# Five weight stages beside the attention's memory, and an expert's weight conversions inside its branch

## The chip, the cores and the metric

One core of one Trainium2 chip runs the whole program in a single launch. The metric is device time in microseconds (us); lower is better. Engines are named as in the profile: PE (matmul) and PEld (weight load), DVE, ACT, POOL, and SP, which issues most DMAs.

## The reference

Three stages follow each other. A windowed attention over 4 batches, 8 heads and 512 local plus 32 global positions gives 2176 tokens of 512 features. A token-shift feed-forward block turns them into `y`. Then comes a mixture of 8 experts, and this is the stage that the change is about:

```python
for b in range(B):
    prev_e = -1
    for s in range(S):
        fresh_e = int(np.argmax(logits[b, s]))
        if s == 0 or local_gate[b, s] < 0.5: e = fresh_e
        else: e = prev_e if prev_e >= 0 else fresh_e
        prev_e = e
        ...                              # p = softmax(logits[b, s])
        h = np.maximum(x[b, s] @ w1[e], 0.0)
        out[b, s] = p[e] * (h @ w2[e])
```

Each expert has `w1` (512x1024) and `w2` (1024x512), together 4 MB in float32.

## The kernel before

Every matmul is made of three passes (`mm3`, L19 to L24): the operands are split into a high part and a rest, and high*high, high*rest and rest*high are summed. So each weight must be converted before it is used. Eight pieces of 512 KB make one expert's weights: pieces 0 to 3 are `w1`, 4 to 7 are `w2`. A piece is loaded by SP into a stage (`part`, L770; a tile of 128x1024), ACT copies it to the high part (L779), and DVE, or POOL for pieces 3 and 7 of each expert (`PP`, L35), subtracts to get the rest (L782). Then the stage is free and SP loads the next piece into it: `whole` and `step` do one conversion and one such load. A load waits on SP until the subtraction of the stage's last piece is done, and SP takes its loads in program order. In what follows `Pk` is the k-th piece, counted over all experts: P8 to P15 belong to the second expert (expert 1), P16 to P23 to expert 2, P24 to P31 to expert 3, and so on.

Three stages (`st0` to `st2`, L1070) lie in a pool on the right side that opens when attention is done (`late`, L727). Two more (`sw0`, `sw1`, L852) are allocated in `alloc`, after the second stage of the program, and SP loads them first inside `run` (`s.fetch()`, L1012). Expert 0's eight pieces are converted during the feed-forward block, so the expert stage begins with P8 to P10 in `st` and P11, P12 on their way to `sw`.

While expert e is computed, expert e+1's eight pieces are converted:

- Experts 0 and 1 run `one` (L941), for one chunk of 128 tokens. `tall` (L899) computes the hidden layer with tokens as the stationary operand: two halves `b`, each 12 matmuls; the relu of a half (L918) goes to `hs`, `turn` transposes it back (L904) and ACT and DVE evacuate it (L906, L907). Conversions stand at `TW`: three before the first half (L909), one after its relu (L919), one at the turn inside the second half (L915). The other three go into `product` (L923), after steps 2, 4 and 6 of 8.
- Experts 2 to 6 run `expert` (L961). Nested branches on the token count `c` pick a side: `joined(N)` computes N=256, 288, 320 or 352 tokens at once, `big` 256 and then more, `single` one chunk, `none` nothing. Behind the branches stands a common tail (L998 to L1000): a `product` of 24 matmuls with bank 0. Five conversions stand in the side, three of them in `wide` (L887, after the relus of steps 2, 4, 6 by `FW`) and two in the next products, and three in the tail (L999). In the profiled execution the relus' shapes show that expert 2 runs `joined(288)`, experts 3 and 4 run `big`, expert 5 `joined(352)` and expert 6 `joined(256)`.
- Expert 7 runs `one` without conversions.

Inside the expert stage each engine's order is the order of the program text. Each engine evaluates the branches itself. PE's sequencer runs ahead of its array: it executes a branch while matmuls that stand before it are still queued.

Of the kernel before, what the change touches and what calls it, by code (L numbers as in the profile page):

```python
# [10 lines left out]
F32=mybir.dt.float32; F32R=mybir.dt.float32r; BF=mybir.dt.bfloat16; I32=mybir.dt.int32  # L11
AF=mybir.ActivationFunctionType; ALU=mybir.AluOpType; X=mybir.AxisListType.X
PSUM=bass.MemoryType.PSUM; DRAM=bass.MemoryType.DRAM
P=128; D=512; F=1024; E=8; SG=32; SL=512; S=544; NB=4; T=2176; HD=64; NK=9; NCH=17
# [4 lines left out]
def mm3(nc,out,wh,wl,xh,xl,first,last,order=None):  # L19

    i=nc.tensor.matmul(out,wh,xh,start=first,stop=False)  # L21
    if order: order(i)
    nc.tensor.matmul(out,wh,xl,start=False,stop=False)  # L23
    return nc.tensor.matmul(out,wl,xh,start=False,stop=last)  # L24
# [7 lines left out]
GA=6; PA=6  # L32
ND=[k for k,n in enumerate([1, 5, 5, 11, 3, 4, 6, 16]) for _ in range(n)]
V7=[1,1,2,2,3,3,3,3]
PP=(0,0,0,1,0,0,0,1); TW=(1,1,1,(2,4,6),3)  # L35
NR=4; NP=4
FX=(3,5,7); WJ=(288,320,352); MW=352; FW=(2,4,6); NW=(2,3); NST=2
def tiles(n): return 4*n-3
LAT=0.2; DLAT=2.1; SLACK=dict(P=0.15,A=0,D=0,G=0)
def op(e,d,need=(),free=(),when=None): return e,d,need,free,when  # L40
# [1 line left out]
class Sched:  # L42
# [11 lines left out]
    def one(s):  # L54

        for x in sorted(s.L,key=lambda x:(s.t<x[3]+(SLACK.get(x[2][0],0) if x[4] else 0),x[0])):
            e,d,need,free,when=x[2]
            if x[3]>s.t or (e and s.busy[e]>s.t) or any(s.places[k]<need.count(k) for k in need) or (when and not when()): continue
            for k in need: s.places[k]-=1
            if e:  # L60
                end=s.t+d; s.busy[e]=end; later=end+(DLAT if e in "QW" else LAT)
                s.left+=[(later,k) for k in free]
            s.next(x)
            if e: same=x[2] and x[2][0]==e; x[3]=end if same else later; x[4]=not same
            return True
# [686 lines left out]
class Experts:  # L752
# [19 lines left out]
    def split(s,e,which,q,st,pool=False):  # L772
# [4 lines left out]
        else:  # L777
            yield "A",.95
            nc.scalar.activation(h[:,qs],st,AF.Copy)  # L779
        if not pool: pool=PP[4*which+q]  # L780
        yield ("G",2.46) if pool else ("D",1.14)
# [67 lines left out]
    def alloc(s):  # L849
        w=s.work  # L850

        new=[s.xwork.tile([P,1024],F32,name=f"sw{i}",bufs=1) for i in range(NST)]  # L852
        s.x=[[s.xwork.tile([P,4,512],F32R,name=f"x{q}{i}",bufs=1) for q in "hl"] for i in range(2)]
        s.h=[w.tile([P,8,MW],F32R,name=f"h{q}",bufs=1) for q in "hl"]
        s.at=w.tile([P,2],I32,name="at",bufs=1); s.by=w.tile([P,2],F32,name="by",bufs=1)
        s.bank=[s.ps.tile([P,512],F32,tag=f"po{i}",name=f"po{i}",bufs=1) for i in range(2)]
        s.st+=new; s.free+=new
    def rows(s,i,n=256): return [t[:,:,i[1]:i[1]+n] for t in s.x[i[0]]]
    def row(s,e,k):

# [26 lines left out]
    def wide(s,i,e,N,W=(),X=()):  # L887

        nc=s.nc; W=list(W); X=list(X); w1h,w1l=s.views(e,0); xh,xl=s.rows(i,N); hh,hl=[t[:,:,:N] for t in s.h]
        for f in range(8):  # L890
# [4 lines left out]
            nc.vector.scalar_tensor_tensor(out=hl[:,f],in0=ph,scalar=0.0,in1=hh[:,f].bitcast(F32),op0=ALU.max,op1=ALU.subtract)  # L895
            if f in FX: s.go(X)
            if f in FW: s.go(W)
        s.go(X,8); s.go(W,8)
    def tall(s,i,e,W=(),X=None):  # L899

        nc=s.nc; W=list(W); w1h,w1l=s.views(e,0); xh,xl=s.rows(i); hh,hl=s.h
        def turn(b):
            pt=s.ps.tile([P,4,P],F32,tag="ph",name="pht2",bufs=4)
            for f in range(4): nc.tensor.transpose(pt[:,f],hs[b][:,f*P:(f+1)*P],s.ident)  # L904
            sl=slice(4*b,4*b+4)
            nc.scalar.activation(hh[:,sl,:P],pt,AF.Copy)  # L906
            nc.vector.tensor_sub(hl[:,sl,:P],pt,hh[:,sl,:P].bitcast(F32))  # L907
        hs=[]
        s.go(W,TW[4])  # L909
        for b in range(2):  # L910
            ph=s.ps.tile([P,512],F32,tag="ph",name="pht",bufs=4)
            bs=slice(b*512,(b+1)*512)
            for d in range(4):
                if b and d==2:
                    turn(0); s.go(W,TW[1])  # L915
                mm3(nc,ph,xh[:,d,:P],xl[:,d,:P],w1h[:,d,bs],w1l[:,d,bs],d==0,d==3)
            hs.append(s.work.tile([P,512],F32,tag="osb",name="hs",bufs=2))
            nc.scalar.activation(hs[b],ph,AF.Relu)  # L918
            if b==0: s.go(W,TW[0])  # L919
        if X is None: return lambda: turn(1)  # L920
        for f in X: f()
        s.go(W,8); turn(1)
# [18 lines left out]
    def one(s,i,e,b,W,X,o=None):  # L941

        W=list(W); last=s.tall(i,e,[W.pop(0) for _ in range(min(5,len(W)))])
        g=dict((f,[]) for f in range(8)); g[TW[2]].append(last)
        for f,x in zip((0,3,4),X): g[f].insert(0,x)
        for f,w in zip(TW[3],W): g[f].append(w)
        s.product(b,e,slice(0,P),g); s.place(b,*s.cols(e,0),o=o)
    def more(s,i,e,k,c,d=0):

# [10 lines left out]
            with two.Else(): single()  # L960
    def expert(s,i,i2,e,c,rows,own,X,third):  # L961

        tc=s.tc; keep=s.loaded,list(s.staged),list(s.free); W=[s.whole]*5
        def begin(k=0,early=True):
            s.loaded,s.staged,s.free=keep[0],list(keep[1]),list(keep[2])
            ch=e*NCH+s.o[e]+2*k
            s.nc.gpsimd.tensor_copy(s.at,s.idx[:,ch:ch+2]); s.nc.gpsimd.tensor_copy(s.by,s.pcol[:,ch:ch+2])
            if early: rows()
        def second(W): s.product(1,e,slice(P,2*P),dict(zip((0,2),([w] for w in W))))
        def big():  # L970
            begin(1,False)
            s.wide(i,e,256,W[:3],[own,lambda: (rows(),X[0]()),X[1]])
            s.out_(0,e,0,slice(0,P),{2:W[:1]}); s.out_(1,e,1,slice(P,2*P),{2:W[:1]})
            with tc.If(c>=tiles(4)) as four:
                s.wide(i2,e,256); second([])
            with four.Else(): s.tall(i2,e,[],[])
        def joined(N):
            begin()
            s.wide(i,e,N,W[:3],X)
            if N>256: s.out_(0,e,2,slice(256,N))  # L980
            second(W[:2])
        def single():
            begin(); s.tall(i,e,W,X)
        def none():
            begin()
            for g in (*W,*X): g()
        L=WJ
        def chain(k):
            if k==len(L): big(); return
            with tc.If(c>=tiles(3)+k+1) as up: chain(k+1)  # L990
            with up.Else(): joined(L[k])
        with tc.If(c>=tiles(2)) as two:
            with tc.If(c>=tiles(3)) as up: chain(0)
            with up.Else(): joined(256)
        with two.Else():
            with tc.If(c>=1) as some: single()
            with some.Else(): none()
        s.place(1,s.by[:,1:2],s.at[:,1:2])  # L998
        s.product(0,e,slice(0,P),{1:[third],2:[s.whole],4:[s.whole],6:[s.whole]})  # L999
        s.place(0,s.by[:,0:1],s.at[:,0:1])  # L1000
    def run(s):
        tc=s.tc; K=s.K
# [52 lines left out]
def program(tc,ins,out):  # L1055
    nc=tc.nc
    with ExitStack() as ctx:
        p=lambda n,**k: ctx.enter_context(tc.tile_pool(name=n,bufs=1,**k))
        const=p("const")
        y=p("dram",space=DRAM).tile([T+1,D],F32,name="y")  # L1060
        ident=const.tile([P,P],F32,name="ident"); make_identity(nc,ident)
        pair=lambda pool,i: [pool.tile([P,4096],F32R,tag=f"slot{i}{q}",name=f"slot{i}{q}") for q in "hl"]
        wp=p("wp"); slots=[pair(wp,0)]
        early=[wp.tile([P,4096],t,tag="slot1"+q,name="early"+q) for q,t in (("h",I32),("l",F32))]
        def place():
            slots.append(pair(wp,1)); return slots[1]
        x=Experts(tc,ident,ins['moe2_w1'],ins['moe2_w2'],y,out,slots)
        def right():
            r=p("right",side="right")
            x.st=[r.tile([P,1024],F32,name=f"st{i}") for i in range(3)]  # L1070
            x.xs=[r.tile([P,2,D],F32,name=f"xs{i}") for i in range(x.K)]
            t=pair(r,2); x.free=list(x.st); x.fetch(); return t
        with ExitStack() as st:
            m=phase1(tc,st,ins,const,y,ident,x,slots,early,place,right)
            x.idx,x.pcol,x.counts,x.cmax=m.idx,m.acc[:,E*NCH:],m.ci,m.cm

        t=dict(reuse_waits="tile")
        x.xwork=p("xwork",**t); x.work=p("work",**t); x.ps=Pools("pt",p("pst",space=PSUM,**t),p("ps2",space=PSUM,**t))
        x.alloc()
        slots.append(pair(p("wq",**t),3))  # L1080
        with tc.manual_schedule():
            x.run()
# [23 lines left out]
```

## Time and profile before

| | |
|---|---|
| three runs | 773.02, 768.14, 772.2 us (median 772.2) |
| the profiled execution | 773.22 us, of which its span is 771.5 us |
| mean granted TensorE clock | 0.973 |
| PE busy | 94% of the span |
| DVE, ACT, POOL busy | 64%, 51%, 45% |
| DMA | 99 GB/s over the span |
| loads of expert weights | 42 into `st`, 22 into `sw` |

The span is the time from the first to the last instruction. PE is busy nearly all the time, so a change shows in the stretches in which it is not. The chain of waits that ended last covers only the last microseconds here and says nothing on the expert stage, so the idle entries on PE's own timeline are read instead, and what each of them waited for. Attention and the feed-forward block fill the first 535 us, the experts the rest.

### The profile page before, as it was taken

The page shows a single profiled execution, that of the slowest core. Times are in us where ns is not written, and L with a number is a line of the kernel's source. Part 1 is how long each engine was busy: PE and PEld are TensorE (multiplying, and loading weights), DVE is VectorE, ACT ScalarE, POOL GpSimd, SP SyncE. Part 2 cuts the span into 40 slices and gives each one's busy share as a digit, 9 for nine tenths or more (in the row PEclk, how much of TensorE's full clock was granted, in tenths as well). Part 3 has the DMA queues.
Part 4 walks back from the last instruction along what each step waited for, and adds up shares of the span by engine and source line. Part 5 has one row for each costly group of instructions (what it writes and reads, how often), then busy time and mean ns, then how long its engine had stood idle before and what let it go on. Part 6 is the DMA issues. An engine that isn't in the chain of part 4 may idle for free. (4 is left out here: it accounts for less than half of the span.)

```text
span 771.5 us, 13972 instructions
## 1 busy us (share of the span) xinstructions
PE 726.4 (94%) x4702; PEld 611.4 (79%) x4702; DVE 496.9 (64%) x1477; ACT 389.9 (51%) x974; POOL 345.0 (45%) x480
## 2 busy tenths in 40 slices
PE   5888888999999999999999899999989999999997
PEld 3555676889898888898888789777777998889795
DVE  6698878968578587587675693577754624435361
ACT  4787566665265565464664442243643613334251
POOL 5566858644626346437245251211643422404421
PEclk9997799999999999999999999999999999999999
DMA  6585133121210321211110320042884633606530
GB/s 150 134 239 147 58 77 107 42 66 23 65 43 3 79 53 24 73 37 40 42 24 14 123 83 28 19 146 65 314 292 137 240 120 109 205 30 193 165 129 24
DMA packets 93185, 76.37 MB, mean 99 GB/s; under 512 B 70350, under 2 KB 74446, under 8 KB 93074
## 3 DMA queue, kind: packets, MB, share of 16 engines
q1 hardware_dynamic: 89618, 64.27, 28.0%
q0 software_dynamic: 3456, 10.75, 4.1%
q8 instruction: 53, 0.87, 0.5%
q14 instruction: 58, 0.48, 0.2%
HBM read 66.08 MB, written 9.44 MB: 98 GB/s over the span
## 5 line engine op out<-in xcount | busy, mean ns | idle before, releaser
L223 POOL TENSOR_SCALAR pl<-pl,mx 128x192 f32<-128x192 f32 (+1 forms) x128 | 64.0, 512 | 86.1 <-DVE mx L220 40.5
L217 ACT ACTIVATE pl<-pl,mx 128x224 f32<-128x224 f32 (+1 forms) x128 | 58.8, 461 | 34.8 <-DVE mx L214 28.0
L21 PE MATMUL psk<-xs,slot0h 128*128 128x256 f32 x256 | 74.6, 297 | 0.8 <-ACT xs L447 0.8
L23 PE MATMUL psk<-xs,slot0h 128*128 128x256 f32 x256 | 73.6, 289 | 0.0
L24 PE MATMUL psk<-xs,slot0l 128*128 128x256 f32 x256 | 73.4, 288 | 0.0
L449 POOL TENSOR_TENSOR xs<-xm,xs 128x512 fp32r<-128x512 f32 (+1 forms) x36 | 46.7, 1309 | 40.2 <-ACT xs L447 40.2
L894 ACT ACTIVATE hh<-ph 128x256 fp32r<-128x256 f32 (+2 forms) x56 | 22.4, 400 | 76.3 <-PE ph L24 45.9
L442 POOL TENSOR_SCALAR xm<-xT,mut 128x256 f32<-128x256 f32 (+7 forms) x96 | 42.7, 461 | 36.8 <-DVE xT L293 17.9
L21 PE MATMUL psv<-slot1h,kh 128*128 128x512 f32 x136 | 55.3, 406 | 0.0
L23 PE MATMUL psv<-slot1l,kh 128*128 128x512 f32 x136 | 54.3, 400 | 0.0
L24 PE MATMUL psv<-slot1h,kl 128*128 128x512 f32 x136 | 54.2, 398 | 0.0
L895 DVE SCALAR_TENSOR_TENSOR hl<-ph,hh 128x256 fp32r<-128x256 f32 (+2 forms) x56 | 24.7, 442 | 44.2 <-ACT hh L894 42.2
L229 PE MATMUL ptp<-ident,pl 128*128 128x128 f32 x256 | 44.1, 292 | 6.8 <-DVE qT L120 1.3
L21 PEld LDWEIGHTS psk<-xs,slot0h 128*128 128x128 f32 x256 | 48.9, 194 | 1.8 <-ACT xs L447 0.9
L23 PEld LDWEIGHTS psk<-xs,slot0h 128*128 128x128 f32 x256 | 48.9, 191 | 1.2
L24 PEld LDWEIGHTS psk<-xs,slot0l 128*128 128x128 f32 x256 | 48.9, 191 | 0.6
L237 PE MATMUL av<-ph,v 128*128 128x256 f32 x192 | 44.7, 293 | 2.2 <-DVE xT L293 1.8
L866 POOL DMA_INDIRECT xs<-y,idx x23 | 24.8, 1078 | 46.9 <-PE pt L873 22.4
L445 DVE SCALAR_TENSOR_TENSOR xm<-xT,mut,xm 128x256 f32<-128x256 f32 (+7 forms) x96 | 41.4, 464 | 3.2 <-POOL xm L442 3.0
L120 DVE TENSOR_TENSOR plo<-ptp,ph 128x512 fp32r<-128x512 f32 x48 | 32.7, 685 | 14.9 <-ACT ph L118 14.7
L21 PE MATMUL ph<-xh,slot2h 128*128 128x256 f32 (+1 forms) x128 | 37.9, 296 | 4.2 <-issue 4.2
L229 PEld LDWEIGHTS ptp<-ident,pl 128*128 128x128 f32 x256 | 30.6, 148 | 13.8 <-issue 3.3
(740 smaller groups left out, 2396.5 us busy)
## 6 DMA issues: line engine op xcount, KB each, us to landing
st<-in_moe_w_dram SPq DMA_DIRECT2D x42, 512.0 KB
sw<-in_moe_w_dram SPq DMA_DIRECT2D x22, 512.0 KB
y<-r SPq DMA_DIRECT2D x17, 256.0 KB
qn<-in_q_l_dram SPq DMA_DIRECT2D x32, 128.0 KB
kn<-in_k_l_dram SPq DMA_DIRECT2D x32, 128.0 KB
earlyh<-in_moe_w_k_dram SPq DMA_DIRECT2D x8, 512.0 KB
raw<-in_moe_w_v_dram SPq DMA_DIRECT2D x8, 512.0 KB
vn<-in_v_l_dram SPq DMA_DIRECT2D x24, 96.0 KB
```

Of the source, the lines that this page charges most:

```text
L21: i=nc.tensor.matmul(out,wh,xh,start=first,stop=False)
L23: nc.tensor.matmul(out,wh,xl,start=False,stop=False)
L24: return nc.tensor.matmul(out,wl,xh,start=False,stop=last)
L120: nc.vector.tensor_sub(out[1],x,out[0].bitcast(F32))
L217: nc.scalar.activation(p[:,h,ks],p[:,h,ks],AF.Exp,bias=mx[:,h:h+1],scale=-1.0,accum_out=mx[:,4+h:5+h])
L223: nc.gpsimd.tensor_scalar(out=p[:,h,ks],in0=p[:,h,ks],scalar1=mx[:,6+h:7+h],scalar2=0.0,op0=ALU.mult,op1=ALU.add)
L229: nc.tensor.transpose(pt[:,c,h],p[:,h,c*96:c*96+P],s.ident)
L237: nc.tensor.matmul(o,s.v(u,x,i,c),P_[y][:,c],start=c==m==0,stop=c==1 and m==len(parts)-1)
L442: nc.gpsimd.tensor_scalar(out=x[:,u,o:o+k],in0=s.xT[b][:,c,q:q+k],scalar1=m[:,1,c:c+1],scalar2=0.0,op0=ALU.mult,op1=ALU.add)
L445: nc.vector.scalar_tensor_tensor(out=x[:,u,o:o+k],in0=s.xT[b][:,c,1+q:1+q+k],scalar=m[:,0,c:c+1],in1=x[:,u,o:o+k],op0=ALU.mult,op1=ALU.add)
L449: nc.gpsimd.tensor_sub(xl[:,cs,:n],x[:,:,:n],xh[:,cs,:n].bitcast(F32))
L866: s.nc.gpsimd.indirect_dma_start(out=s.xs[i][:,j,:],out_offset=None,in_=s.y,in_offset=IndirectOffsetOnAxis(ap=s.idx[:,ch:ch+1],axis=0))
```

## The change

- `NST` stages are no longer allocated in `alloc`. All five lie in the right pool, so all five are loaded as soon as attention is done. When the expert stage begins, P8 to P12 are staged, and `run`'s `fetch` has nothing to do.
- Expert 1's `tall` converts one piece at its start, one after the first half's relu, two at the turn and one after the second half's relu, instead of three, one and one. Expert 0's places stay.
- All eight conversions of experts 2 to 6 stand inside the side. `wide` has places after steps 1, 2, 4, 6 and 7: five are taken by `joined(256)`, four by the wider ones, three by `big`. The rest go into the products of the side. The tail keeps only the preparation of a token chunk (`third`).

```diff
-PP=(0,0,0,1,0,0,0,1); TW=(1,1,1,(2,4,6),3)
+PP=(0,0,0,1,0,0,0,1); TW=((3,1,1,0),(1,1,2,1)); TF=(2,4,6)
-FX=(3,5,7); WJ=(288,320,352); MW=352; FW=(2,4,6); NW=(2,3); NST=2
+FX=(3,5,7); WJ=(288,320,352); MW=352; FW=(1,2,4,6,7); NST=2
...
-        new=[s.xwork.tile([P,1024],F32,name=f"sw{i}",bufs=1) for i in range(NST)]
-        s.st+=new; s.free+=new
...
-        s.go(W,TW[4])
+        n=TW[e>0]
+        s.go(W,n[0])
...
-                    turn(0); s.go(W,TW[1])
+                    turn(0); s.go(W,n[2])
...
-            if b==0: s.go(W,TW[0])
+            s.go(W,n[1+2*b])
...
-        tc=s.tc; keep=s.loaded,list(s.staged),list(s.free); W=[s.whole]*5
+        tc=s.tc; keep=s.loaded,list(s.staged),list(s.free); W=[s.whole]*8
-        def second(W): s.product(1,e,slice(P,2*P),dict(zip((0,2),([w] for w in W))))
+        def second(W): s.product(1,e,slice(P,2*P),{0:W[:1],1:W[1:2],2:W[2:]})
-            s.out_(0,e,0,slice(0,P),{2:W[:1]}); s.out_(1,e,1,slice(P,2*P),{2:W[:1]})
+            s.out_(0,e,0,slice(0,P),{0:W[:1],2:W[:1],4:W[:1]}); s.out_(1,e,1,slice(P,2*P),{0:W[:1],2:W[:1]})
-            s.wide(i,e,N,W[:3],X)
-            if N>256: s.out_(0,e,2,slice(256,N))
-            second(W[:2])
+            s.wide(i,e,N,W[:5 if N==256 else 4],X)
+            if N>256: s.out_(0,e,2,slice(256,N),{0:W[:1],2:W[:1],4:W[:1]})
+            second(W[:3 if N==256 else 1])
-        s.product(0,e,slice(0,P),{1:[third],2:[s.whole],4:[s.whole],6:[s.whole]})
+        s.product(0,e,slice(0,P),{1:[third]})
...
-            x.st=[r.tile([P,1024],F32,name=f"st{i}") for i in range(3)]
+            x.st=[r.tile([P,1024],F32,name=f"st{i}") for i in range(3+NST)]
```

## Rows read from the trace of the kernel before

**Rows 1.** PE's timeline, expert stage: start us, duration us, instruction, [idle before <-releaser]

```profile
555.98 0.65 PE L904 MATMUL pht<-ident,hs 128*128 128x128 f32 x4 [1.84 <-ACT slot2h L779]
560.58 0.66 PE L904 MATMUL pht<-ident,hs 128*128 128x128 f32 x4 [0.54 <-ACT hs L918]
569.08 0.58 PE L21 MATMUL ph<-xh,slot2h 128*128 128x288 f32 x1 [2.77 <-issue]
...
695.74 0.40 PE L21 MATMUL ph<-xh,slot1h 128*128 128x352 f32 x1 [0.35 <-issue]
...
730.77 0.39 PE L21 MATMUL ph<-xh,slot2h 128*128 128x256 f32 x1 [1.41 <-issue]
```

**Rows 2.** PE's branch instructions by line: duration ns min/median/max, first and last start us

```profile
L990 PEldq COMPARE_BRANCH  x1: 5790/5790/5790, 563.1 to 563.1; - x1
L990 PEldq COMPARE_BRANCH  x1: 3700/3700/3700, 591.2 to 591.2; - x1
L990 PEldq COMPARE_BRANCH  x1: 3913/3913/3913, 691.7 to 691.7; - x1
L990 PEldq COMPARE_BRANCH  x1: 3679/3679/3679, 719.0 to 719.0; - x1
L993 PEldq COMPARE_BRANCH  x1: 5532/5532/5532, 725.2 to 725.2; - x1
```

**Rows 3.** Busy by stretch: us, engines (instructions), granted clock, DMA share, GB/s

```profile
568.90:572.20 3.30, 3.12 (x13) 3.15 (x14) 0.00 (x0) 0.00 (x0) 2.86 (x5) 0.50 0.90 283
591.00:595.00 4.00, 4.00 (x19) 3.24 (x18) 0.85 (x1) 0.00 (x0) 3.98 (x2) 1.00 0.06 14
596.00:600.00 4.00, 4.00 (x21) 3.25 (x21) 2.10 (x3) 2.62 (x4) 1.02 (x1) 1.00 0.95 317
564.00:568.00 4.00, 2.31 (x11) 1.56 (x9) 3.26 (x5) 2.60 (x3) 2.79 (x3) 1.00 1.03 409
724.00:728.00 4.00, 4.00 (x21) 3.28 (x20) 2.09 (x4) 2.78 (x4) 1.03 (x1) 1.00 0.89 226
```

**Rows 4.** DMA queues, 563.2 to 566.45, 566.45 to 567, 592 to 593: packets, MB, share

```profile
q1 hardware_dynamic: 412, 1.29, 99.0%
...
q8 instruction: 1, 0.02, 12.0%
...
q8 instruction: 1, 0.02, 8.8%
```

**Rows 5.** DMA queues, 725.3 to 728.1, then 728.1 to 728.2

```profile
q1 hardware_dynamic: 154, 0.57, 87.6%
...
q8 instruction: 1, 0.02, 55.8%
```

**Rows 6.** SP's timeline: weight loads before the entry of expert 6

```profile
722.99 2.18 SPq L770 DMA_DIRECT2D sw<-in_moe_w_dram  x2
```

**Rows 7.** ACT's timeline, expert 1

```profile
554.38 1.06 ACT L779 ACTIVATE slot2h<-st 128x1024 fp32r<-128x1024 f32 x1 [2.68 <-DMA st<-in_moe_w_dram]
555.34 0.58 ACT L918 ACTIVATE hs<-pht 128x512 f32<-128x512 f32 x1
...
558.98 1.06 ACT L779 ACTIVATE slot0h<-st 128x1024 fp32r<-128x1024 f32 x1 [1.35 <-DMA st<-in_moe_w_dram]
559.95 0.58 ACT L918 ACTIVATE hs<-pht 128x512 f32<-128x512 f32 x1
...
561.27 0.60 ACT L906 ACTIVATE hh<-pht 128x512 fp32r<-128x512 f32 x1 [0.25 <-PE pht L904]
```

**Rows 8.** ACT's timeline, experts 2 (to 597.87) and 5

```profile
583.16 1.05 ACT L779 ACTIVATE slot1h<-sw 128x1024 fp32r<-128x1024 f32 x1
...
584.76 1.05 ACT L779 ACTIVATE slot1h<-sw 128x1024 fp32r<-128x1024 f32 x1
585.71 1.05 ACT L779 ACTIVATE slot3h<-st 128x1024 fp32r<-128x1024 f32 x1
...
597.87 2.00 ACT L779 ACTIVATE slot3h<-st 128x1024 fp32r<-128x1024 f32 x2
...
710.72 1.05 ACT L779 ACTIVATE slot2h<-st 128x1024 fp32r<-128x1024 f32 x1
```

**Rows 9.** POOL's and DVE's timelines, subtractions that overlap

```profile
550.80 2.43 POOL L782 TENSOR_TENSOR slot3l<-st,slot3h 128x1024 fp32r<-128x1024 f32 x1
...
550.75 4.70 DVE L782 TENSOR_TENSOR slot2l<-sw,slot2h 128x1024 fp32r<-128x1024 f32 x2
```

More of the change, by code (lines that the diff above doesn't have):

```diff
@@ L943, in one @@
         W=list(W); last=s.tall(i,e,[W.pop(0) for _ in range(min(5,len(W)))])
-        g=dict((f,[]) for f in range(8)); g[TW[2]].append(last)
+        g=dict((f,[]) for f in range(8)); g[1].append(last)
         for f,x in zip((0,3,4),X): g[f].insert(0,x)
-        for f,w in zip(TW[3],W): g[f].append(w)
+        for f,w in zip(TF,W): g[f].append(w)
         s.product(b,e,slice(0,P),g); s.place(b,*s.cols(e,0),o=o)
```

## The prediction

> **What bounds the kernel now.** PE is busy nearly all the time, so I read its own timeline in the expert stage first, for every idle entry over 0.3 us. There are five [rows 1]. Two stand in expert 1 (1.84 and 0.54 us) and end with ACT's conversion or the relu behind it. Three stand at the first matmul after a branch: at the entry of expert 2 (2.77 us), of expert 5 (0.35 us) and of expert 6 (1.41 us). Their releaser is "issue", that is, no semaphore. Together they are 6.91 us, 0.9% of the span.
>
> So the second view is PE's branch instructions [rows 2]. Those shown jump, and the sequencer gets its next instructions after 3.7 to 5.8 us. PE hides this as long as queued matmuls last. Branch time less idle time gives how long they last: 5.79-2.77 = 3.0 us, 3.91-0.35 = 3.6 us, 5.53-1.41 = 4.1 us. The jumps out of a side at 591.2 (3.70 us) and 719.0 (3.68 us) leave no idle entry.
>
> Third, why a jump takes 3.7 us or 5.8 us. Where DMA was nearly idle, 591 to 595 with a share of 0.06 [rows 3], the instruction queue's packet came between 592 and 593 and the jump of 591.2 took 3.70 us. At 563.1 the loads' queue took 99% of the DMA engines' time and no instruction packet came until after 566.45 [rows 4]; the jump was done 2.4 us after that. At 725.2 it was the same: no packet until 728.1 [rows 5], and two weight loads had been issued just before, from 722.99 to 725.2 [rows 6]. I read this so: an instruction fetch stands behind the loads issued before it. Two loads then hold a fetch for 5.1 us after the first one's issue (728.1-722.99), and PE has its instructions 2.4 us later. The idle time at 569.08 also costs clock: from 568.9 to 572.2 the granted clock was 0.50, the lower level of 1.2 GHz [rows 3], so at most half of 3.3 us, 1.65 us.
>
> **The change part by part.**
>
> *Five stages early.* Two 512 KB loads move from the start of the expert stage to the end of attention. P11 and P12 need no wait at expert 0, but no idle PE entry stands there, so this is worth nothing by itself. The two loads stand on SP ahead of nothing that is due then; I take 0. Phase one's order may shift with them; no row prices that, and I allow 1 us either way.
>
> *Expert 1.* ACT's third conversion at the start waits 2.68 us for its load [rows 7], and the first half's relu, which is ready, is queued behind it (555.34). PE waits for that relu, 1.84 us. With one conversion at the start the relu runs in time and this wait goes. Likewise the fifth conversion now waits 1.35 us for its load ahead of the second relu, and PE waits 0.54 us; after the change it stands behind that relu. What is late next: this fifth conversion (P20) still waits for its load, which lands at about 559, because its stage is freed by POOL in expert 0 and that does not move. Behind it ACT queues the next chunk's evacuation and the second turn's evacuation (561.27), and the product's fifth step needs the latter. The chain is 558.98 + 1.06 + 0.59 + 0.60 = 561.2, against 561.87 now [rows 7]. So of 2.4 us I count 0.7 us as a gain by the end of expert 1. Bounds: 0 and 2.4.
>
> *Entry of expert 2.* Expert 1's later pieces load as before and the DMA engines are full (share 1.03 from 564 to 568 [rows 3]); the fetch stands behind the same loads and PE only reaches the branch earlier. So I count the 0.7 us as the whole gain of experts 0 and 1 together, if PE starts expert 2 0.7 us sooner, and nothing for the 2.77 us. Bounds: 0, and all of 1.84+0.54+2.77+1.65 = 6.8 us.
>
> *The tail without conversions.* Expert 2's tail now starts its three conversions at 597.87 [rows 8]; in the change they run earlier. Before the entry of expert 5 no load is in flight: 0.35 us goes. Before the entry of expert 6, of the two loads from 722.99 one remains (P55's stage comes from POOL after the scatter, as P51's does now), so the fetch is held about half as long and 1.41 us goes. Sum 1.76 us. Bounds: 0 and 1.76.
>
> *The sides with conversions.* ACT does not wait for PE between conversions. In expert 2 the third one starts at 583.16, and two follow at once from 584.76 on [rows 8]. After the change the fourth stands at 583.16 (step 6 of `wide`), and four more run back to back, 0.95 us apart, until about 588.6. The fourth is POOL's: it subtracts from 584.2 to 586.6, 2.43 us. DVE does not get on beside it: two subtractions that started with POOL's took 4.70 us, 2.43 plus two of 1.1 [rows 9]. So stages come free at 586.6, 587.7, 588.8 and 590.0, and four loads (2.1 MB) stand ahead of the jump at 591.2. Now the DMA engines are idle there, with the share of 0.06. Price: two loads hold a fetch 5.1 us; two more at the 317 GB/s of 596 to 600 [rows 3] add 3.3 us. The fetch comes at 586.6+8.4 = 595.0, PE has its instructions at 597.4, the jump takes 6.2 us, and with matmuls for 4.1 us the new idle time is 2.1 us. In expert 5 the fourth conversion stands at 710.72; loads go out at 714.2, 715.3, 716.4 and 717.5; 714.2+8.4+2.4 = 725.0 against 719.0+4.1: 1.9 us. Sum 4.0 us. Lower bound: all four at 409 GB/s [rows 3] and 1 us to start, 6.1 us, which gives 0 at both. Upper bound: at 226 GB/s, 10.2 us, 3.9+3.7 = 7.6 us, and twice 1.65 us if the clock falls: 10.9 us. I take the middle rate, as it is that of loads into freed stages in this very expert. `big` converts at least 15 us before its exit; no price. `joined(256)` loads no further expert; no price.
>
> The DMA engines' order is what the sum hangs on. The Trainium skill (DMA: Bandwidth & Descriptors, "Queues, rings and completion order") says that each DMA engine goes round its queues packet by packet. By that rule a fetch would not stand behind loads, and the sum would be that of rival three. The gaps without a packet in [rows 4, 5] speak against it.
>
> *Sum.* -0.7 - 1.76 + 4.0 = +1.5 us. The profiled execution took 773.22 us, with a span of 771.5, so it becomes 774.7 with a span of 773.0; the median of the runs is 1.0 us lower, so 773.7 us. A measurement here tells about 1%, 7.7 us, from no change.
>
> **The rivals.** One: *everything goes and the exits stay hidden.* PE gains 6.8+1.76 = 8.6 us: 763.6 us. For it: the removed waits are on PE itself. Against it: the load of P20 and the full DMA engines up to 575 do not change. It needs expert 1's loads to land about 3 us sooner.
>
> Two: *the exits become the bound*, slower than before. It decides from about 3 us of idle time each, where the clock falls too, as it did after 2.77 us but not after 1.84 us: 10.9-1.76 = +9.1 us, 781.3 us. For it: 226 GB/s was seen with loads into the same kind of stage. Against it: nothing else is on the queues at 591 and 719.
>
> Three: *the fetch does not stand behind the loads.* Then neither the entries gain nor the exits lose; only the 0.7 us of expert 1 remains: 771.5 us.
>
> Four: *exits hidden, expert 1 as I have it*: -0.7-1.76: 769.7 us. For it: at 409 GB/s the price is 0.
>
> **How the numbers follow.** Forecast 0.45, rival one 0.12, two 0.08, three 0.15, four 0.20. The likeliest is 773.7 us, with its own range of 771 to 777. Leaving out one and two, which are 0.2 together, the range is 767.0 to 778.5: rival four less a part of the entry's 2.77 us, and the forecast with the exits' upper price but no fall of the clock, 773.7+3.6, and 1 us for phase one. Faster by over 1% (below 764.5) is rival one alone, 0.12; slower by over 1% is rival two, 0.08; the rest, 0.80, is within 1%.
>
> **What the profile would show.** Right: the 1.84 us entry gone, and PE's idle entries at experts 5 and 6 gone, with their jumps near 3.7 us; new idle entries of about 2 us at the first matmul of the tails of experts 2 and 5, with jumps near 6 us and a DMA share near 1 there. Wrong: exits that still take 3.7 us beside loads in flight (the reading of the queue falls), expert 2's entry without idle time (the loads were not the limit), or stretches before 535 us that differ by over 1 us.

## Result and profile after

| | before | after |
|---|---|---|
| median (range) of 17 runs each, us | 770.97 (765.42 to 775.4) | 777.9 (773.48 to 783.24) |
| ratio | | 1.0093, 95% interval 1.0072 to 1.0114 |
| profiled execution, us (span) | 773.22 (771.5) | 779.77 (778.0) |

The ratio is a loss of about 7.2 us (0.0093 x 771), between 5.6 and 8.8. Forecast were +1.5 us and 773.7 us, with a range of 767.0 to 778.5: the time lies inside the range and within 1%, but close to the upper edge, and above the 771 to 777 of the likeliest case.

Spans can't be compared here: the first matmul of the expert stage stands at 532.0 to 538.7 us in the executions shown here, with hardly a difference in the program ahead of it. So I cut the expert stage at the first matmul of experts 2, 3, 5, 6 and 7 on PE's timeline and compare its parts (us). Each row is one execution, and the idle time before a cut counts to the part ahead of it:

| kernel | experts 0, 1 | 2 | 3, 4 | 5 | 6 | 7 to end | stage |
|---|---|---|---|---|---|---|---|
| before | 32.31 | 32.26 | 94.40 | 35.03 | 23.08 | 17.65 | 234.73 |
| after | 32.97 | 34.75 | 94.23 | 35.47 | 27.31 | 17.69 | 242.42 |
| early stages alone | 32.63 | 32.37 | 94.37 | 34.25 | 23.07 | 17.64 | 234.33 |
| conversions in the sides alone | 31.38 | 32.88 | 94.21 | 34.47 | 27.47 | 18.23 | 238.64 |
| after, tail as before | 32.89 | 32.38 | 94.25 | 35.28 | 23.07 | 18.27 | 236.14 |
| after, half loads | 30.73 | 31.19 | 94.19 | 33.59 | 27.39 | 17.76 | 234.85 |
| after, three conversions less | 33.62 | 34.42 | 94.51 | 34.41 | 23.08 | 18.02 | 238.06 |
| dense | 32.49 | 31.13 | 94.24 | 33.70 | 23.09 | 17.95 | 232.60 |
| dense exits only | 33.31 | 32.36 | 94.40 | 33.64 | 27.47 | 17.50 | 238.68 |

The stage is 7.69 us longer after the change: 4.23 in expert 6, 2.49 in expert 2, 0.66 in experts 0 and 1, 0.44 in expert 5. PE's timeline, as in [rows 1], names the places (lines after the change stand one or two lower: the branch of L990 is L989):

```profile
559.54 0.50 PE L21 MATMUL po<-slot3h,hh 128*128 128x512 f32 x1 [0.30 <-ACT hh L904]
561.98 0.80 PE L24 MATMUL po<-slot3h,hl 128*128 128x512 f32 x1 [1.71 <-DVE hl L905]
568.58 0.41 PE L21 MATMUL ph<-xh,slot2h 128*128 128x288 f32 x1 [2.02 <-issue]
...
597.24 0.47 PE L21 MATMUL po<-slot0h,hh 128*128 128x512 f32 x1 [2.13 <-issue]
...
697.56 0.40 PE L21 MATMUL ph<-xh,slot1h 128*128 128x352 f32 x1 [0.18 <-issue]
...
726.93 0.47 PE L21 MATMUL po<-slot3h,hh 128*128 128x512 f32 x1 [1.76 <-issue]
...
753.19 0.77 PE L21 MATMUL po<-slot0h,hh 128*128 128x512 f32 x1 [2.59 <-DVE slot3l L782]
```

Of the five waits of [rows 1], the two of expert 1 and those at the entries of experts 5 and 6 are gone or small. Four new ones stand there: PE's wait for DVE's `hl` in expert 1, the first matmuls of the tails of experts 2 and 5, and the largest at the tail of expert 6. PE's branches, as in [rows 2]:

```profile
L989 PEldq COMPARE_BRANCH  x1: 5990/5990/5990, 562.4 to 562.4; - x1
L989 PEldq COMPARE_BRANCH  x1: 6280/6280/6280, 590.8 to 590.8; - x1
L989 PEldq COMPARE_BRANCH  x1: 3790/3790/3790, 693.6 to 693.6; - x1
L989 PEldq COMPARE_BRANCH  x1: 5914/5914/5914, 720.9 to 720.9; - x1
L992 PEldq COMPARE_BRANCH  x1: 3422/3422/3422, 729.0 to 729.0; - x1
```

The exits at 590.8 and 720.9 went from 3.7 to 6.28 and 5.91 us, the entry of expert 6 from 5.53 to 3.42. Busy by stretch, columns as in [rows 3]:

```profile
561.94:565.36 3.42, 3.38 (x10) 2.81 (x11) 2.60 (x4) 1.69 (x3) 0.88 (x1) 0.50 1.01 385
568.80:572.20 3.40, 3.40 (x16) 3.40 (x16) 0.00 (x0) 0.39 (x1) 2.92 (x5) 0.50 0.83 280
590.00:596.00 6.00, 5.12 (x22) 3.78 (x21) 0.32 (x1) 0.00 (x0) 3.32 (x2) 1.00 0.83 265
597.20:600.60 3.40, 3.36 (x17) 2.82 (x18) 1.06 (x2) 0.60 (x1) 1.00 (x1) 1.00 0.22 83
753.10:756.50 3.40, 3.31 (x8) 2.66 (x9) 0.75 (x1) 0.00 (x0) 0.99 (x1) 0.50 0.14 54
```

The granted clock falls to the lower level, 0.50, behind the waits at 561.98, 568.58 and 753.19, but not behind the exit of expert 2, where it is 1.00 from 597.2 on.

How the exit of expert 2 became late can be read off SP's timeline and the queues. The four loads stand ahead of the jump at 590.8:

```profile
586.33 3.69 SPq L770 DMA_DIRECT2D st<-in_moe_w_dram  x4
```

The queues from 590.8 to 594.5 (first line) and from 590.8 to 594.7 (the others):

```profile
q1 hardware_dynamic: 305, 1.11, 82.1%
...
q1 hardware_dynamic: 311, 1.11, 78.2%
q8 instruction: 1, 0.02, 1.6%
...
q14 instruction: 2, 0.02, 1.4%
```

No packet of q8, the queue whose packets are shown in [rows 4, 5], comes for 3.7 us; it comes when the loads' 1.11 MB are through, and the jump is done 2.4 to 2.6 us later (590.8 + 6.28 = 597.1). That is the mechanism of [rows 4, 5] at a new place. Two packets of another instruction queue, q14, did come between 592 and 594, while the loads took 80 to 90% of the DMA engines' time. So the loads do not hold up every fetch; whether PE's stands strictly behind them or only loses to them is not shown.

### The profile page after: what moved, and what is told of

It is laid out like the page before. It is cut to its first block, busy times and chain, and to the rows that moved or that the text cites. A ratio compares the mean times of both kernels' runs of the same rounds, so it can differ in the third digit from the quotient of the medians.

```text
span 778.0 us, 13964 instructions
## 1 busy us (share of the span) xinstructions
PE 728.1 (94%) x4702; PEld 612.7 (79%) x4702; DVE 505.6 (65%) x1477; ACT 389.8 (50%) x974; POOL 341.8 (44%) x480
## 5 line engine op out<-in xcount | busy, mean ns | idle before, releaser
L864 POOL DMA_INDIRECT xs<-y,idx x23 | 27.7, 1203 | 54.2 <-PE pt L871 22.2
```

The lines of the kernel that those rows point to most:

```text
L864: s.nc.gpsimd.indirect_dma_start(out=s.xs[i][:,j,:],out_offset=None,in_=s.y,in_offset=IndirectOffsetOnAxis(ap=s.idx[:,ch:ch+1],axis=0))
```

## Experiments

### The two halves of the change

**Early stages alone.** The kernel before, with the five stages in the late pool.

```diff
-        new=[s.xwork.tile([P,1024],F32,name=f"sw{i}",bufs=1) for i in range(NST)]
...
-        s.st+=new; s.free+=new
...
-            x.st=[r.tile([P,1024],F32,name=f"st{i}") for i in range(3)]
+            x.st=[r.tile([P,1024],F32,name=f"st{i}") for i in range(3+NST)]
```

> The kernel before with one part of the change alone: all five stages lie in the right pool and are loaded when attention is done; the places of the conversions stay. My theory: the two early loads hide, and P11 and P12 never held PE, so the time stays within 0.3% of before (about 771 us), and the start of the expert stage moves by less than 1 us against the end of attention. Rival: the loss lies in phase one, because the two loads and the moved tiles change the order there; then this kernel alone is slower by 2 us or more and the stretch from the end of attention to the first expert grows.

Measured: 770.24 us beside 770.96, ratio 0.9989 (0.9959 to 1.0020). The exits take 3.4 us and have no idle time.

**Conversions in the sides alone.** The changed kernel with its stages back at their old place and expert 1's conversions at the old places.

```diff
-TW=((3,1,1,0),(1,1,2,1))
+TW=((3,1,1,0),(3,1,1,0))
...
+        new=[s.xwork.tile([P,1024],F32,name=f"sw{i}",bufs=1) for i in range(NST)]
...
+        s.st+=new; s.free+=new
...
-            x.st=[r.tile([P,1024],F32,name=f"st{i}") for i in range(3+NST)]
+            x.st=[r.tile([P,1024],F32,name=f"st{i}") for i in range(3)]
```

> The kernel before with the other part alone: all conversions of experts 2 to 6 inside their sides, stages and expert 1 as before. My theory: this part carries the whole loss. New idle entries of PE of about 2 us each at the first matmul of the tails of experts 2 and 5 (jumps near 6 us), 2.6 us at the tail of expert 6 with a stretch at the lower clock behind it (1.4 us), against 1.76 us gained at the entries of experts 5 and 6: about +6 us, 777 us. Expert 1 keeps its 1.84 and 0.54 us. Rival: the loss comes from the stages or from expert 1; then this kernel is within 2 us of before.

Measured: 780.09 us, ratio 1.0110 (1.0051 to 1.0168). By the time, this half alone costs what the whole change does, within a wide interval. Its one trace shows less: the stage is 3.91 us longer than before, of which expert 6 makes 4.39. PE idles 1.77 us at the exit of expert 2 but only 0.54 at that of expert 5, where 2 had been expected, and at the entry of expert 2 the clock stays high.

**After, tail as before.** Early stages and expert 1's new places stay, the conversions go back into the tail.

```diff
-FW=(1,2,4,6,7)
+FW=(2,4,6)
...
-            second(W[:3 if N==256 else 1])
+            second(W[:2])
...
-        s.product(0,e,slice(0,P),{1:[third]})
+        s.product(0,e,slice(0,P),{1:[third],2:[s.whole],4:[s.whole],6:[s.whole]})
```

> The kernel after with the tail undone: five early stages and fewer conversions at the start of expert 1, but five conversions in the side and three in the tail as before. My theory: expert 1 trades 2.4 us of idle time for about 2 us (the third pass of the product's fifth step waits for a subtraction queued behind P20's) and 1.4 us at the lower clock, and the entry of expert 2 takes up the rest: 771 us, within 2 us of before; entries of experts 5 and 6 keep 0.35 and 1.4 us, exits stay near 3.7 us. Rival: expert 1's new places cost by themselves, then it is 3 us or more slower than before.

Measured: 771.5 us, ratio 0.9990 (0.9958 to 1.0022). What follows from the three: the loss comes with the conversions in the sides. The stages are worth nothing that these runs can tell, as forecast, and expert 1's places show neither a gain nor a loss: its step of 32.89 us lies beside 32.63 with the old ones.

### Does a fetch stand behind the loads?

The changed kernel, but from the second expert's weights on, a load brings half of its piece.

```diff
+        if s.loaded>=8: o,v=(o[:,:,:512],v[:,:,:512]) if c==1 else (o[:,:1],v[:,:1])
```

> The kernel after, but each weight load from P8 on moves only half of its 512 KB (half of each piece's columns or rows is left as an older piece left it), so this leaves out half of the weights' loading; conversions, matmuls and branches are all there. My theory, that PE's instruction fetch stands behind the loads: the jumps out of experts 2 and 5 fall from 6.3 and 5.9 us to 4.5 us or less, their idle entries of 2.13 and 1.76 us fall below 0.5 us, and the jump into expert 2 falls by more than 1 us. Rival, that the jumps are longer because the sides have more instructions or because of where the code lies: they stay near 6 us.

Measured: 768.69 us in one run. The jumps into expert 2 and out of experts 2 and 5 (the same branch, here L991):

```profile
L991 PEldq COMPARE_BRANCH  x1: 3690/3690/3690, 558.8 to 558.8; - x1
L991 PEldq COMPARE_BRANCH  x1: 4340/4340/4340, 583.4 to 583.4; - x1
L991 PEldq COMPARE_BRANCH  x1: 4034/4034/4034, 711.4 to 711.4; - x1
```

They were 5.99, 6.28 and 5.91 us, and PE has no idle entry over 0.3 us at any of the three places. In three more kernels with full loads and the change's sides for experts 2 and 5 (conversions in the sides alone, three conversions less, P20 later) the two exits take 5.92 to 6.14 and 4.69 to 5.03 us. The order of the engines' work is the same and only the bytes ahead of the fetch are fewer, so the fetch waits for them: rival three falls. The queues after the jump at 558.8, until 559.8 and until 560.3, show the packet coming in the half microsecond in which the loads stop:

```profile
q1 hardware_dynamic: 96, 0.17, 55.5%
...
q1 hardware_dynamic: 102, 0.18, 38.5%
q8 instruction: 1, 0.02, 4.1%
```

### Expert 6's tail

On DVE and POOL the side of expert 6 ends after the change so:

```profile
746.43 6.61 DVE L782 TENSOR_TENSOR slot3l<-st,slot3h 128x1024 fp32r<-128x1024 f32 x3 [0.53 <-ACT slot3h L779]
...
745.06 2.41 POOL L782 TENSOR_TENSOR slot1l<-st,slot1h 128x1024 fp32r<-128x1024 f32 x1 [7.72 <-ACT slot1h L779]
749.32 2.65 POOL L782 TENSOR_TENSOR slot3l<-st,slot3h 128x1024 fp32r<-128x1024 f32 x1 [1.85 <-ACT slot3h L779]
```

DVE is done with the last of the three at 753.04, and PE's wait ends at 753.19. POOL ended its own at 751.97; the last of DVE's, which started at 749.61 beside it, took 3.44 us. But the matmul that waits reads `slot0h` and `hh`, which were there long before. To test whether the wait is for these conversions, the next kernel ("three conversions less" in the table) leaves out the last three conversions of that side.

```diff
-            second(W[:3 if N==256 else 1])
+            second(W[:0 if N==256 else 1])
```

> The kernel after, but expert 6's side leaves out its last three conversions (the last three pieces of expert 7's second matrix keep an older expert's values); everything else is there. My theory: the 2.59 us that PE waits at the first matmul of expert 6's tail end with DVE's last subtraction of the side, although that matmul reads nothing that it writes, because behind the branches one count of DVE's work stands for the whole side. Without the three, DVE's last work of the side ends about 4 us sooner: the idle entry and the lower clock behind it are gone, expert 7 starts about 4 us sooner after expert 6's first matmul (23.3 us instead of 27.3). Rival: PE waits there for its bank or for its own jump; then the entry stays at 2 us or more.

Measured: 777.5 us in one run, and expert 6's step is 23.08 us, as before the change. Around the tail's first matmul, now at 752.20, PE has no idle time and the full clock (columns as above):

```profile
747.00:750.00 3.00, 3.00 (x15) 2.44 (x14) 2.24 (x2) 1.16 (x2) 2.22 (x1) 1.00 0.29 109
750.00:753.00 3.00, 3.00 (x15) 2.42 (x14) 0.85 (x2) 0.00 (x0) 0.00 (x0) 1.00 0.02 5
```

So the first matmul behind the branches of expert 6 waits for conversions that it does not read. That DVE's part of them is what it waits for is read from the trace, where DVE ends last. The price is 27.31 - 23.08 = 4.23 us: 2.59 us of waiting, and the rest from the fall of the clock behind it. In the kernel with P20 later, below, the same wait is 2.56 us, the clock stays at 1.00 and expert 6 takes 25.86 us.

### Expert 1

ACT's chain, which I had priced, is early after the change. What comes last is DVE's:

```profile
557.46 1.06 ACT L779 ACTIVATE slot0h<-st 128x1024 fp32r<-128x1024 f32 x1 [0.79 <-DMA st<-in_moe_w_dram]
...
558.90 0.59 ACT L904 ACTIVATE hh<-pht 128x512 fp32r<-128x512 f32 x1
...
558.55 2.18 DVE L782 TENSOR_TENSOR slot0l<-st,slot0h 128x1024 fp32r<-128x1024 f32 x1 [2.15 <-ACT slot0h L779]
560.65 0.68 DVE L874 TENSOR_TENSOR xl<-pt,xh 128x512 fp32r<-128x512 f32 x1
561.25 0.68 DVE L905 TENSOR_TENSOR hl<-pht,hh 128x512 fp32r<-128x512 f32 x1
561.85 1.27 DVE L782 TENSOR_TENSOR slot0l<-st,slot0h 128x1024 fp32r<-128x1024 f32 x1
...
557.25 2.39 POOL L782 TENSOR_TENSOR slot2l<-st,slot2h 128x1024 fp32r<-128x1024 f32 x1
```

POOL subtracts from 557.25 to 559.64. DVE's subtraction for P20 starts at 558.55 and ends at 560.73, 1.09 us after POOL's; the next one alone takes 1.27 us. Behind it queue `xl` and `hl`, and PE waits 1.71 us for `hl`; then the clock is at 0.50 for 3.42 us (from 561.94). The wait comes with the new places: five more traces with them and P20 not moved show it, with 1.48 to 2.30 us and a lower clock behind it, and none of the four with the old places does. The Trainium skill (SBUF — State Buffer, "Terms") says that DVE and GpSimd, the profile's POOL, arbitrate for one pair of ports that is held for a whole instruction, and that the loser stands still. These rows agree: 1.09 us are left to do after POOL's end, close to the 1.27 us of the one alone.

**P20 later.** The changed kernel with P20 behind the second turn's evacuation.

```diff
-TW=((3,1,1,0),(1,1,2,1))
+TW=((3,1,1,0),(1,1,2,0))
...
-        W=list(W); last=s.tall(i,e,[W.pop(0) for _ in range(min(5,len(W)))])
+        W=list(W); last=s.tall(i,e,[W.pop(0) for _ in range(min(5-(e>0),len(W)))])
...
```

> The kernel after with one conversion of expert 1 (P20) moved from behind the second relu to behind the second turn's evacuation. My theory: the 1.71 us at the product's fifth step come from DVE, which subtracts for P20 while POOL holds it up and evacuates the turn only after that; with P20 behind it the entry falls below 0.5 us and the clock stays high there. The jump into expert 2 waits for the loads all the same, so expert 2 starts at most 1.5 us sooner after expert 0's first matmul (now 33.0 us). Rival: the evacuation waits for ACT or for the gather; then the idle time stays over 1 us. Second rival: the entry follows in full, and expert 2 starts 3 us sooner.

Measured: 780.47 us in one run. The wait for `hl` is gone, so its cause was as read; but nothing is won:

```profile
563.55 0.63 PE L879 MATMUL pt<-ident,xs 128*128 128x128 f32 x4 [1.48 <-DMA xs<-y,idx]
...
570.69 0.58 PE L21 MATMUL ph<-xh,slot2h 128*128 128x288 f32 x1 [4.41 <-issue]
```

PE waits for the gather of the next rows instead, and the entry of expert 2 takes all that it was early: experts 0 and 1 take 33.02 us, beside 32.97. What frees PE earlier in expert 1 is given back here at the fetch behind the loads: the entry's idle time is 4.41 us instead of 2.02.

### A version without the two prices

**Dense.** If the exits cost because loads go out just ahead of the jump, and the tail because conversions stand at the end of the side, both should go when all eight conversions of a joined side stand in its first half, one after each relu.

```diff
-FW=(1,2,4,6,7)
+FW=tuple(range(8))
...
-            s.wide(i,e,N,W[:5 if N==256 else 4],X)
-            if N>256: s.out_(0,e,2,slice(256,N),{0:W[:1],2:W[:1],4:W[:1]})
-            second(W[:3 if N==256 else 1])
+            s.wide(i,e,N,W,X)
+            if N>256: s.out_(0,e,2,slice(256,N))
+            second([])
```

> The kernel after with all eight conversions of a joined side inside its wide, one after each step, and none in the products that follow. If the loads are what holds the jumps, the last load of experts 2 and 5 is issued some 3 us sooner and is through when PE jumps: jumps out of 4.3 us or less, no idle entry at their tails. DVE's last work of expert 6 ends before the tail: no idle entry there either. Together 2.1 + 1.8 + 2.6 + 1.4 = 7.9 us less than after: about 770 us, the time of before. Rival: ACT and DVE have not the time for a conversion at every step (1.44 us of PE at 256 tokens against 1.45 us of ACT and 1.64 us of DVE), the relus come late, and PE waits for a bank in wide: then 2 us or more of new idle time stand in the wides of experts 2, 5 and 6.

Measured: 768.82 us beside 773.06, ratio 0.9956 (0.9925 to 0.9987): 0.4% faster than the kernel before, and clear of the changed kernel's 1.0093. SP's last loads before the exit of expert 2, and the jumps out of experts 2 and 5:

```profile
579.48 4.18 SPq L770 DMA_DIRECT2D st<-in_moe_w_dram  x3
```

```profile
L989 PEldq COMPARE_BRANCH  x1: 4180/4180/4180, 585.8 to 585.8; - x1
L989 PEldq COMPARE_BRANCH  x1: 3854/3854/3854, 713.8 to 713.8; - x1
```

The last load is out by 583.66, 2.1 us before the jump; after the change it was 590.02, 0.8 us before. PE has two waits left:

```profile
558.98 0.67 PE L24 MATMUL po<-slot3h,hl 128*128 128x512 f32 x1 [1.88 <-DVE hl L905]
565.14 0.37 PE L21 MATMUL ph<-xh,slot2h 128*128 128x288 f32 x1 [1.54 <-issue]
```

**Dense exits only.** Experts 2 and 5 dense, expert 6's side as the change has it.

```diff
-            if f in FW: s.go(W)
+            if f in FW or N>256: s.go(W)
...
-            s.wide(i,e,N,W[:5 if N==256 else 4],X)
+            s.wide(i,e,N,W[:5 if N==256 else 8],X)
...
```

> The changed kernel with the eight conversions of experts 2 and 5 all in the first half of their sides, and expert 6's side left as the change has it (five in its first half, three in its second). Theory: the price of the exits and that of the join in expert 6 are apart and add up. The steps of experts 2 and 5 then come out at 31.1 and 33.7 us, as in the dense kernel, without idle time at their exits; expert 6's step stays at 27.3 us, with 2.6 us of idle time for DVE at the second product and the fall of the clock behind it; the expert stage takes 232.6 + 4.2 = 236.8 us, about 773 us in all, a ratio near 1.001. Rival: expert 6's wait comes from what the late exits push into it (POOL and DVE behind their loads); then it goes with them, its step takes 23.1 us, and the time is the dense kernel's, a ratio of 0.9955.

Measured: 776.29 us beside 771.8, ratio 1.0041 (1.0010 to 1.0072). The exits have no idle time, expert 6's step stays at 27.47 us, and its wait is the same:

```profile
570.88 0.58 PE L21 MATMUL ph<-xh,slot2h 128*128 128x288 f32 x1 [2.42 <-issue]
...
751.54 0.72 PE L21 MATMUL po<-slot0h,hh 128*128 128x512 f32 x1 [2.60 <-DVE slot3l L782]
```

So the two prices are apart and add up. The stage missed its forecast of 236.8 by 1.9 us, mostly because the entry of expert 2 was idle for 2.42 us instead of 1.54 (experts 0 and 1: 33.31 instead of 32.49) and the clock fell behind it (expert 2: 32.36 instead of 31.13).

**Dense, with expert 1 changed again.** Two more kernels put expert 1's conversions elsewhere in the dense kernel: P20 later, as above, and all at the places of before.

> The two edits before together: all eight conversions of a joined side inside its wide, and P20 of expert 1 behind the second turn's evacuation. If both idle times are taken away and the entry of expert 2 gives back half of the second: about 769 us, some 2 us less than before. If the entry takes all: 770 us. Rival as before: new waits inside the wides, 772 us or more.

Measured: 772.25 us beside 773.06, ratio 0.9986 (0.9955 to 1.0016), stage 233.68 us. The gain of some 2 us that was expected is not shown: the wait for the gather is 1.69 us, the entry of expert 2 idles for 3.83, and the clock falls there.

> The dense kernel (all eight conversions of a joined side within its first half), with expert 1's conversions at the places that they had in the kernel before (three at the start, then one, one, none). Theory: expert 1 loses as much by the new places (DVE's subtraction, held by POOL, ahead of the last turn) as it gains on ACT, so experts 0 and 1 together take the 32.2 us of the run with the five early stages alone, or up to 0.7 us less than in the dense kernel, and the rest of the expert stage is the dense kernel's: 232 us for the stage, ratio to the kernel before about 0.995. Rival: expert 1's new places are a gain, which is lost only with late stages: then experts 0 and 1 take over 33.3 us with the old places, and the stage 233 us or more. In either case the exits of experts 2 and 5 jump in about 4 us with no idle time, and expert 6's tail has none.

Measured: 772.52 us beside 771.8, ratio 0.9998 (0.9969 to 1.0026), stage 235.04 us. Experts 0 and 1 take 32.88 us, between what the two theories said; the relu's wait of before is back with 2.45 us, the entry of expert 2 idles for 2.19 us, and the clock falls behind both. Neither theory is borne out cleanly. Of the three placements the change's own gives the shortest stage in the dense kernel, but the ratios' intervals overlap.

## Why the prediction was right, and where its sum was not

Against the sum, term by term (us, from the table of parts):

| term | forecast | measured |
|---|---|---|
| experts 0 and 1 | -0.7 | +0.66 |
| entries of experts 5 and 6 | -1.76 | -0.17 (experts 3, 4) and -1.41 = -1.58 |
| exits of experts 2 and 5 | +4.0 | 2.49 + (0.44 + 1.41) = +4.34 |
| `joined(256)` | no price | +4.23 |
| expert 7 | none | +0.04 |
| sum | +1.5 | +7.69 |

*The exits: right at expert 2, and at expert 5 in this execution.* POOL's subtraction ended at 586.29 (forecast 586.6), the four loads went out from 586.33 to 590.02 (586.6 to 590.0), the packet came between 594.5 and 594.7 (595.0), the jump took 6.28 us (6.2) and PE idled for 2.13 us (2.1); at expert 5, 1.76 us (1.9). The middle rate fits. The clock did not fall at either. The other three kernels with the same sides idle 1.77 to 1.99 us at expert 2, but only 0.54 to 0.88 at expert 5, so the 1.9 us there came true in one execution of four; why it varies stays open. Rival two asked for about 3 us of idle time at each exit and did not come; rival four needed hidden exits and fell with these rows.

*The entries of experts 5 and 6: right.* 0.18 us and nothing are left, with jumps of 3.79 and 3.42 us. The 0.35 us at expert 5 is too small to be sure of: with three conversions less its entry idles for 0.45 us.

*`joined(256)`: the step that failed.* "Loads no further expert; no price" looked only at loads. Three conversions moved into the last product of that side, and DVE, held by POOL, ends them 2.4 us after PE has run out of work. The prediction asked what a moved conversion issues, but not who waits at the join for the engine that does it. This term alone is two thirds of the 6.2 us that the sum lacked.

*Expert 1: right about the wait that went, wrong about what is late next.* The 1.84 us are gone: four traces with the old places have 0.84 to 2.45 us at that matmul, and none with the new ones has over 0.3. I named ACT's chain as the next and made it end at 561.2; it was early, because its load was waited for 0.79 us only, and DVE's chain came last. [rows 9] already held the price: a DVE subtraction beside POOL's takes the longer time, and I used that for the exits and not here. The sum also had no term for the clock, which fell behind the new wait of 1.71 us: half of 3.42 us at the lower level is 1.7 us at most. The error is 1.36 us.

*Entry of expert 2: right in kind.* 2.02 us are left of 2.77 and the clock still falls; a kernel with the same code there (three conversions less) idles for 2.78 us, so the difference says nothing. As forecast, what PE gains in expert 1 is not kept; rival one needed it kept.

*Phase one* stays open: its term of 0, 1 us either way, is below what these executions scatter by. The sign of being wrong that it names, over 1 us ahead of 535, can't be read for the same reason: the stage starts at 536.77 us before and at 535.61 after.

That the time fell within 1% and within the range was luck in part: two terms were mis-sized in the same direction, and the range held it because it reached for the upper price of the exits, which did not come. It also rested on 772.2 us, the median of three runs of the kernel before; all 17 give 770.97, and +1.5 on that would have been 772.5.

## What to carry to other kernels

Where a program branches at run time, look for the last load issued before each jump: here 2 MB put out within the last 4.5 us before it added about 2 us of PE idle time at the exit of expert 2, and with the last four loads spread over the 8.4 us before it, the last out 2.1 us ahead, none over 0.3 us was left. When work moves ahead of a join, list every engine that does part of it and ask when the slowest ends, as the first instruction behind the join may wait for all of it. And where a wait is removed, follow the queue of each engine that feeds the same matmul, not only of the one that was last.

## What the runs showed of the hardware that I had not expected

- A jump took 3.4 to 3.8 us where no weight load stood ahead of it (3.42 and 3.79 us after the change, 3.70 and 3.68 us before), so even then PE lives on the matmuls that are queued. The Trainium skill (Runtime: NRT & Kernel Launch, "Instruction fetch mechanics") says that a taken branch out of the window fetched in advance stalls until the target has been fetched; the trace agrees: at the jump of 729.0 a packet of q8 comes between 730 and 731, and the jump ends at 732.4.
- Idle time of about the same length does not always lower the clock: behind 2.02 us at the entry of expert 2 it was 0.50, behind 2.13 us at its exit it stayed at 1.00. At the entry another fall, behind the wait for `hl`, had ended 3.2 us before. Behind the wait at the tail of expert 6 it was 0.50 after 2.59 us and, with P20 later, 1.00 after 2.56. These rows give no rule for when it falls.
